# Stores of whole tiles issued by SyncE instead of ScalarE in a decode-attention backward kernel

## The chip, the cores and the metric

The kernel runs on one core of a Trainium2 chip. The metric is the device time of one execution in microseconds (us). Of three runs of the kernel before, the median is 1286.4 us, the lowest 1285.06 and the highest 1288.95.

## The reference

Softmax attention with one query row a head, and its gradients. There are B x H = 2 x 32 = 64 heads, 8192 keys a head, and D = 128; all arrays are bf16.

```
def _fwd_reference(q, k, v):
    scale = q.shape[-1] ** -0.5
    scores = jnp.einsum("bhqd,bhkd->bhqk", q, k) * scale
    p = _softmax(scores, axis=-1)
    return jnp.einsum("bhqk,bhkd->bhqd", p, v)

def reference(q, k, v, grad_out):
    ...
    _out, _vjp = jax.vjp(_f, q, k, v)
    _grads = _vjp(grad_out)
    return (_out, *_grads)
```

So for each head the kernel reads K and V (2 MB each) and writes dK and dV (2 MB each): dV is the outer product of the weights p with grad_out, dK that of the weights' gradient dS with q. The output and dq are one row of 128 values a head.

## The kernel before

A head's K and V lie in SBUF as tiles `kt` and `vt` of 128 partitions x 64 rows x 128 values, 16 KB a partition, 2 MB in all. Each of the two has five buffers (`UNITS = 5`, line 67).

`load(h)` (line 97) issues two DMAs from SyncE (the profile calls it SP), K first, then V; each fills a whole tile. Five heads are loaded ahead of the loop.

The main loop (from line 353) makes 65 rounds. Round h does two things interleaved in eight steps j of two halves: the scores of head h (y in the code) and the gradients of head p = h - 1 (x).

- For head h, TensorE transposes K (steps 0 to 3) and V (steps 4 to 7) in groups of eight 128 x 128 blocks into PSUM (`transposes`, line 113). ScalarE copies each group to SBUF (line 120); in two of the sixteen halves VectorE does (line 118). TensorE then multiplies the copies with q or grad_out (line 136).
- For head p, TensorE sums the weighted rows (line 241) in steps 0 to 3, and VectorE writes the outer products (`outer`, line 271) over the tile that has been read: `outer(p, w, i)` fills the i-th quarter of tile `kv[1 - w]`. With w = 0 this is dV over V (steps 1 to 3), with w = 1 dK over K (steps 3 to 6).

`store(h, w)` (line 328) then writes the whole tile to HBM with one DMA of 2 MB, issued by ScalarE (line 331). In round h the dV store of head p is issued at step 4 and the dK store at step 7, behind what the program has put in ScalarE's queue before: an engine's queue is served in order, and a store that must wait holds the evictions behind it. The last head is stored in halves of 1 MB.

At step 7, behind the dK store, the program writes `load(h + 3)`. That load takes a buffer of an earlier head and so waits until that head's store has landed. As SyncE has only loads to issue, nothing but such waits holds it.

Every 13th head (6, 19, 32, 45, 58) has its dV stored otherwise: `store_by_fifteen` (line 289) issues 24 small stores from GpSimd (POOL in the profile, line 299), mixed with very small copies (`turn`, line 285). Its rows go to fifteen of the sixteen DMA engines.

The order of instructions on each engine is that of the program (`tc.manual_schedule`, line 353); the framework adds the waits, assigns buffers, and gives each DMA a completion counter.

Of the kernel before, what the change touches and what calls it, by code (L numbers as in the profile page):

```python
# [23 lines left out]
def kernel(  # L24
# [11 lines left out]
    nc = tc.nc  # L36
# [40 lines left out]
    dk_v = out_2.rearrange("b h (p n) d -> (b h) p n d", n=NT)  # L77
    dv_v = out_3.rearrange("b h (p n) d -> (b h) p n d", n=NT)
# [16 lines left out]
    heads = [Head() for _ in range(BH)]  # L95
# [193 lines left out]
    def store_by_fifteen(h, w):  # L289

        dst, src = (dv_v, dk_v)[w][h], heads[h].kv[1 - w]

        def rows(lo, n, step=4, size=8192):
            own = slice(lo, lo + step * (n - 1) + 1, step)
            nc.gpsimd.dma_start(out=dst[own], in_=src[own], max_dma_last_dim=size)  # L299

        def fifth(r):
            rows(16 + r, 2, step=32)

        for r in range(4):

            if r == 1:
                fifth(r)
                turn(14)
            rows(52 + r, 11)
            rows(r, 4, size=16384)  # L310
            if r == 0:
                fifth(r)
                turn(3)
            elif r == 3:
                turn(10)
                fifth(r)
                turn(9)
            else:
                turn(5)
            rows(20 + r, 3)  # L320
            if r == 2:
                fifth(r)
                turn(14)
            rows(96 + r, 8)
            rows(32 + r, 4, size=16384)
            turn(5)

    def store(h, w, a=0, b=NT):
        if (2 * h + w) % RARE == RARE // 2 - 1:
            return store_by_fifteen(h, w)  # L330
        nc.scalar.dma_start(out=(dv_v, dk_v)[w][h][:, a:b, :], in_=heads[h].kv[1 - w][:, a:b, :])

    def outer_and_store(h, w, i):

        outer(h, w, i)
        if h == BH - 1 and i % 2:
            store(h, w, (i - 1) * CH, (i + 1) * CH)
# [15 lines left out]
    with tc.manual_schedule():  # L353
        for h in range(min(UNITS, BH)):
            load(h)
        for h in range(BH + 1):
# [4 lines left out]
            for j in range(NS):  # L361
# [24 lines left out]
                if x and p < BH - 1 and j in (4, 7):  # L386
                    store(p, j // 7)
# [49 lines left out]
```

## Time and profile before

| | |
|---|---|
| median of three runs | 1286.4 us |
| span of the profiled execution | 1285.1 us |
| PE, share busy | 83% |
| ACT, share busy | 71% |
| DVE, share busy | 69% |
| HBM read / written | 268.47 / 268.47 MB |
| mean rate of the DMA engines | 420 GB/s |
| DMA issues by ScalarE | 125 of whole or half tiles, 0.34 us each |
| K load, V load: median to landing | 22.9, 31.5 us |
| dK store, dV store by ScalarE: median to landing | 26.9, 21.9 us |

The profile is one execution. Its page cuts the span into 40 slices of 32.1 us; for each it gives the busy share of the DMA engines in tenths and the rate in GB/s. Queue q1 is SyncE's, q10 ScalarE's, and q0 (software_dynamic) GpSimd's. "From issue to landing" runs from the instruction that issues a DMA to its completion. ACTq and SPq are the sequencers of ScalarE and SyncE, which issue DMAs; the engine itself is not busy meanwhile. A wait is put down to whatever came last before the waiting instruction ran; "issue" is time for which the profile shows no such thing.

### The profile page before, as it was taken

How to read it: one execution, taken by the hardware profiler on the slowest of the kernel's cores; microseconds unless marked ns; L12 is line 12 of the kernel's file. 1: busy time of each engine (PE TensorE's matmuls, PEld its weight loads, DVE VectorE, ACT ScalarE, POOL GpSimd, SP SyncE). 2: the span in 40 equal slices, each digit the busy share in tenths (PEclk: the TensorE clock that was granted, in tenths of full speed). 3: DMA queues.
4: the chain of work that ended last, by engine and by line, in shares of the span. 5: the costliest groups of instructions: out<-in, count | busy, mean ns of one | idle time of the engine just before them, and what ended most of it. 6: DMA issues, size and time to landing. Idle time of an engine off the chain costs nothing.

```text
span 1285.1 us, 42433 instructions
## 1 busy us (share of the span) xinstructions
PE 1060.3 (83%) x18948; PEld 877.3 (68%) x18948; DVE 883.8 (69%) x1511; ACT 909.3 (71%) x1043; POOL 105.8 (8%) x193
## 2 busy tenths in 40 slices
PE   5999888848998799499997984999889849899983
PEld 4777777637777677477776774777767737777772
DVE  1887777737787486378875773787767636778775
ACT  5877778737887586488875774877767736788771
POOL 1000111000002110000021200000111000001120
PEclk9999999969999697799996897998979877999996
DMA  9999999999999999999999999999999999999998
GB/s 396 418 426 428 426 426 425 423 431 427 426 426 426 413 424 427 423 427 425 428 426 399 427 426 418 428 427 428 419 403 426 425 419 391 428 429 425 425 424 336
DMA packets 43879, 539.69 MB, mean 420 GB/s; under 512 B 10192, under 2 KB 10192, under 8 KB 10192
## 3 DMA queue, kind: packets, MB, share of 16 engines
q1 hardware_dynamic: 18432, 268.44, 49.5%
q10 hardware_dynamic: 18320, 258.02, 47.4%
q0 software_dynamic: 6944, 10.51, 2.2%
q8 instruction: 148, 2.42, 0.7%
q14 instruction: 35, 0.29, 0.1%
HBM read 268.47 MB, written 268.47 MB: 418 GB/s over the span
## 4 chain that ended last, share of the span: by engine, by line
PE 40%; DMA 26%; ACT 19%; DVE 11%; issue 3%; ACTq 0%; DVEq 0%; SPq 0%
PE tp L113 23%; ACT ev L120 18%; DMA vt<-in_v_dram 9%; DVE ev L118 9%; DMA out_dram<-vt 9%; PE acc L241 9%; DMA kt<-in_k_dram 4%; PE sm L136 4%; DMA out_dram<-kt 3%; PE dp L206 1%; PE dp L136 1%; PE c L259 1%; DMA nat<-in_grad_out_dram 1%; ACT E_f L175 1%; PE sm L170 1%
## 5 line engine op out<-in xcount | busy, mean ns | idle before, releaser
L120 ACT CAST ev<-tp 128x1024 bf16<-128x1024 f32 x896 | 881.2, 1024 | 335.7 <-PE tp L113 232.3
L113 PE MATMUL tp<-ident_bf,vt 128*128 128x128 bf16 x4096 | 327.4, 225 | 134.7 <-ACT ev L120 121.6
L113 PEld LDWEIGHTS <-vt 128*128 128x128 bf16 x4096 | 268.9, 100 | 167.3 <-issue 153.2
L113 PE MATMUL tp<-ident_bf,kt 128*128 128x128 bf16 x4096 | 335.9, 228 | 17.2 <-DMA kt<-in_k_dram 6.5
L113 PEld LDWEIGHTS <-kt 128*128 128x128 bf16 x4096 | 249.4, 101 | 131.5 <-issue 123.2
L136 PEld LDWEIGHTS <-ev 128*128 128x128 bf16 x8192 | 324.4, 98 | 2.2 <-issue 0.2
L271 DVE TENSOR_TENSOR kt<-qd,dS 128x2048 bf16<-128x2048 bf16 x256 | 310.0, 1212 | 0.0
L271 DVE TENSOR_TENSOR vt<-qd,P 128x2048 bf16<-128x2048 bf16 x256 | 295.8, 1216 | 0.0
L118 DVE CAST ev<-tp 128x1024 bf16<-128x1024 f32 x128 | 156.7, 1224 | 186.4 <-PE tp L113 179.4
L136 PE MATMUL dp<-doT_all,ev 128*128 128x1 bf16 x4096 | 178.5, 164 | 0.1
L136 PE MATMUL sm<-qT_all,ev 128*128 128x1 bf16 x4096 | 176.0, 164 | 0.0
L299 POOL DMA_DIRECT2D out_dram<-vt x120 | 67.0, 560 | 1032.7 <-DVE vt L271 832.1
L241 PE MATMUL acc<-vt,wz 128*32 128x512 bf16 x1024 | 109.3, 418 | 17.8 <-DVE wz L186 17.8
L241 PE MATMUL acc<-kt,wz 128*32 128x512 bf16 x1024 | 103.4, 396 | 0.1
L172 DVE TENSOR_SCALAR negm<-sm 128x1 f32<-128x1 f32 x64 | 9.8, 154 | 108.8 <-PE sm L170 108.8
L241 PEld LDWEIGHTS <-wz 128*32 128x32 bf16 x2048 | 52.8, 93 | 32.1 <-DVE wz L186 22.7
L285 POOL DMA_DIRECT2D spare<-in_q_dram x57 | 34.1, 598 | 121.1 <-DMA out_dram<-vt 107.0
L206 PE MATMUL dp<-ld,ones_f 128*128 128x2 f32 x128 | 25.8, 271 | 21.0 <-DVE ld L193 20.9
L206 PEld LDWEIGHTS dp<-ld,ones_f 128*128 128x128 f32 x128 | 20.6, 202 | 31.1 <-DVE ld L193 31.0
L160 DVE TENSOR_REDUCE mp<-sm 128x1 f32<-128x64 f32 x64 | 14.4, 225 | 36.9 <-PE sm L136 36.9
L211 DVE RECIPROCAL rl_all<-dp 128x1 f32<-128x1 f32 x64 | 10.7, 168 | 32.0 <-PE dp L206 32.0
L170 PE MATMUL sm<-gm,ones_f 1*128 1x1 f32 x128 | 25.8, 268 | 0.0
(42 smaller groups left out, 310.5 us busy)
## 6 DMA issues: line engine op xcount, KB each, us to landing
kt<-in_k_dram SPq DMA_DIRECT2D x64, 2048.0 KB, 22.9
vt<-in_v_dram SPq DMA_DIRECT2D x64, 2048.0 KB, 31.5
out_dram<-kt ACTq DMA_DIRECT2D x63, 2048.0 KB, 26.9
out_dram<-vt ACTq DMA_DIRECT2D x58, 2048.0 KB, 21.9
out_dram<-vt POOLq DMA_DIRECT2D x20, 176.0 KB, 23.2
out_dram<-vt POOLq DMA_DIRECT2D x40, 64.0 KB, 23.0
out_dram<-vt POOLq DMA_DIRECT2D x20, 128.0 KB, 22.6
out_dram<-vt ACTq DMA_DIRECT2D x2, 1024.0 KB, 10.9
```

What stands on the lines that cost most here:

```text
L113: nc.tensor.matmul(tp[:, i, :], lhsT=x.kv[w][:, n, :], rhs=ident_bf[:], start=True, stop=True)
L118: nc.vector.tensor_copy(out=ev[:], in_=tp[:])
L120: nc.scalar.copy(out=ev[:], in_=tp[:])
L136: nc.tensor.matmul((x.dp if w else x.sm)[:, n : n + 1], lhsT=ev[:, i, :], rhs=col, start=True, stop=True,)
L160: nc.vector.reduce_max(out=x.mp[:], in_=x.sm[:, 0:NT], axis=AX.X)
L170: nc.tensor.matmul(mb, lhsT=ones_f[0:1, :], rhs=x.gm[:], start=True, stop=True)
L175: nc.scalar.activation(out=x.E[:], in_=x.sm[:, 0:NT], func=ACT.Exp, bias=negm[:], scale=scale, accum_out=x.ld[:, 0:1],)
L206: nc.tensor.matmul(x.lsum, lhsT=ones_f[:], rhs=x.ld[:], start=True, stop=True)
L241: nc.tensor.matmul(acc[32 * g : 32 * g + 32, :], lhsT=wz[w][k][:, n // 4, :], rhs=rows[:, n : n + 4, :].rearrange("p n d -> p (n d)"), sta ...
L271: nc.vector.tensor_tensor(out=x.kv[1 - w][:, n : n + CH, :].rearrange("p n (d t) -> p n d t", t=2), in0=row.unsqueeze(1).to_broadcast([P, ...
L285: nc.gpsimd.dma_start(out=two(spare[0:n, :])[:, :, i : i + 2], in_=two(q_rows[0:n, :])[:, :, 0:2])
L299: nc.gpsimd.dma_start(out=dst[own], in_=src[own], max_dma_last_dim=size)
```

## The change

One line of `store`: the DMA that stores a whole tile (and the halves of the last head) is issued by SyncE, in the place where the program has it. SyncE's queue then holds, for each round, the dV store, the dK store, and the two loads, in this order. The loads of q and grad_out at the start and the stores of the two small outputs at the end stay with ScalarE, and the stores by fifteen engines with GpSimd.

```
     def store(h, w, a=0, b=NT):
         if (2 * h + w) % RARE == RARE // 2 - 1:
             return store_by_fifteen(h, w)
-        nc.scalar.dma_start(out=(dv_v, dk_v)[w][h][:, a:b, :], in_=heads[h].kv[1 - w][:, a:b, :])
+        nc.sync.dma_start(out=(dv_v, dk_v)[w][h][:, a:b, :], in_=heads[h].kv[1 - w][:, a:b, :])
```

More of the change, by code (lines that the diff above doesn't have):

```diff
@@ L330, in store @@
             return store_by_fifteen(h, w)
-        nc.scalar.dma_start(out=(dv_v, dk_v)[w][h][:, a:b, :], in_=heads[h].kv[1 - w][:, a:b, :])
+        nc.sync.dma_start(out=(dv_v, dk_v)[w][h][:, a:b, :], in_=heads[h].kv[1 - w][:, a:b, :])
     def outer_and_store(h, w, i):
```

## The prediction

> **What bounds the kernel now.** First the page's DMA rows by slice, then its DMA queues, then the stages in windows, then who waits on the store and load queues.
>
> ```profile
> DMA  9999999999999999999999999999999999999998
> GB/s 396 418 426 428 426 426 425 423 431 427 426 426 426 413 424 427 423 427 425 428 426 399 427 426 418 428 427 428 419 403 426 425 419 391 428 429 425 425 424 336
> DMA packets 43879, 539.69 MB, mean 420 GB/s; under 512 B 10192, under 2 KB 10192, under 8 KB 10192
> ...
> q1 hardware_dynamic: 18432, 268.44, 49.5%
> q10 hardware_dynamic: 18320, 258.02, 47.4%
> ```
>
> The 16 DMA engines are taken from end to end, and the rate has a ceiling: four long windows (300 to 400, 540 to 640, 800 to 900, 1100 to 1180 us) give 427 GB/s each. 539.69 MB at 427 GB/s are 1263.9 us of a span of 1285.1 us. So transfers bound the kernel, and the 21 us above that floor are all there is to win: the first two slices and the last fall short of 427 by 31 + 9 + 91, or 131 / 427 x 32.1 = 9.9 us, and the slices between by 149 in sum, 11.2 us.
>
> Where the inner part is lost, by windows (length; busy of PE, PEld, DVE, ACT, POOL; PE clock; DMA share; GB/s):
>
> ```profile
> 531.00:539.00 8.00, 4.19 (x54) 3.98 (x54) 1.29 (x2) 4.59 (x7) 0.00 (x0) 0.50 1.02 410
> ...
> 676.00:688.00 12.00, 4.00 (x52) 3.79 (x52) 1.93 (x3) 4.39 (x7) 2.34 (x5) 0.55 0.92 354
> ...
> 938.00:950.00 12.00, 6.41 (x92) 6.00 (x88) 3.49 (x5) 5.75 (x8) 2.57 (x5) 0.58 0.93 368
> ```
>
> The shortfall against 427 times the length: 0.3, 2.0 and 1.7 us. In the same way 418 to 428 (382 GB/s) 1.1, 791 to 801 (393) 0.8, 921 to 929 (395) 0.6, 1051 to 1062 (390) 0.9, 1074 to 1088 (351) 2.5. Together **9.9 us**, nearly all of the 11.2.
>
> What happens there, in ScalarE's timeline (a store is issued, then an eviction runs that had been idle for the time in brackets):
>
> ```profile
> 533.31 0.34 ACTq L331 DMA_DIRECT2D out_dram<-vt  x1
> 533.74 1.93 ACT L120 CAST ev<-tp 128x1024 bf16<-128x1024 f32 x2 [14.96 <-DMA vt<-in_v_dram]
> ...
> 682.50 0.34 ACTq L331 DMA_DIRECT2D out_dram<-vt  x1
> 682.94 1.93 ACT L120 CAST ev<-tp 128x1024 bf16<-128x1024 f32 x2 [7.87 <-issue]
> ```
>
> and in the chain of waits, in order of time:
>
> ```profile
> 502.64 30.59 DMA vt<-in_v_dram
> ...
> 762.78 30.33 DMA vt<-in_v_dram
> ```
>
> The load of V issued at 502.64 lands at 533.23, and the store of another tile is issued at 533.31. Likewise 762.78 + 30.33 = 793.11 and a store at 793.18; 246.85 + 26.57 = 273.42 and 273.49; 1023.33 + 30.29 = 1053.62 and 1053.69. No data joins the two; I infer a completion counter that both use in turn. A store held at the head of ScalarE's queue holds the evictions behind it, so TensorE stops, the next store is late, and then the next load. The waits on ScalarE put down to loads or to "issue" with such a store ahead are 17.3, 15.0, 15.7, 16.0, 7.8, 7.9 and 5.1 us, 85 us. They cost the end only the dips, since one head without waits takes 17.3 us (stores of V at 198.30 and 215.59) and its four transfers 4 x 2.097 MB / 427 GB/s = 19.6 us (4.9 each).
>
> SyncE's waits (total, times, longest) show what paces the loads, buffers becoming free:
>
> ```profile
> SPq L104 <- DMA out_dram<-kt: 888.6, 57, 40.5
> SPq L104 <- DMA out_dram<-vt: 211.6, 21, 11.9
> ```
>
> **The change part by part.**
> *Removed from ScalarE:* 125 issues (63 + 58 + 2 + 2) of 0.34 us are 42 us of its queue, and the held stores 85 us. Both lie beside the transfers, 19.6 against 17.3 us per head; without that cover they would be worth up to 127 us, here 0 by themselves.
> *Added to SyncE:* as many issues. Four per head are 1.4 us of 19.6, and it otherwise only waits: 0.
> *The dips:* a counter's former user is now always an older transfer of the same queue, and a store that waits holds no eviction. Bounds: 0 (the dips return by another road) to -9.9 us. I take **-8**, four fifths, since the last window (1074 to 1088) follows an earlier hold by one round of loads and may have a part that I can't assign.
> *The order of transfers:* SyncE now issues V store, K store, K load, V load for each head. What queues behind a wait there is every later transfer. (a) In most heads a K load waits for the K store of the head before; behind that store stand two loads and two stores, 4 x 4.9 = 19.6 us, so the queue doesn't run dry. The stores wait for their outer products, which come at the pace of the compute; and that waits for no load, since round h issues the loads of round h + 3, two whole rounds (2 x 17.3 = 34.6 us) ahead, and they land in 23 to 32 us. (b) In the five stretches after a store by fifteen engines the V buffer of that head comes back late, and loads come singly (171.40, 181.69, 192.28 us): the V load waits for the V store of its own round. Only the K store and K load, 9.8 us, then stand behind it. The answer takes 1.0 us from issue to the first bytes (issue at 0.74, first traffic at 1.7 us), and the slowest DMA engine lags: the last 1 MB stores took 11.0 us to land, of which data 2.5 and start 1.0, the rest at most 7.5. 9.8 - 1.0 - 7.5 = +1.3 us in hand: I take 0. As the other bound I let the lag grow by a third, to 10 us: 10 + 1.0 - 9.8 = 1.2 us for each of the 21 waits counted above, +25.
> *Loads and stores in one queue:* not in this trace. Loads alone ran at 426 GB/s (38 to 42 us), stores then loads at 421 and 431 (60 to 66, 66 to 72). The first store after loads alone brought 373 GB/s for 4 us (42 to 46), 0.5 us; the store at 273.49 brought none (426, then 434). So a turn costs between 0 and 0.5 us, x 62 heads = 0 to +31. I take 0, by the later row, since both directions were then already running.
> *GpSimd's stores:* unchanged in number. They share the engines with one queue instead of two and should end sooner than now (144 to 252 us for the first); nothing waits for that: 0.
> *The end:* last four half stores 10.9 to 11.0 us to landing as before: 0, within 2 us.
>
> Sum against the profiled execution: 1285.1 - 8 = 1277.1. That execution lies 1.3 us below the median of the three runs, 1286.4; so the median should fall to 1278.4, **say 1279 us**.
>
> **The rivals.**
> *No change (1286).* The dips' cause is the imbalance among DMA engines, not held stores; then the work of the slowest decides and the order of issue nothing. For it: DMA share 1.00 at 393 GB/s in 791 to 801. Against it: shares of 0.92 and 0.93 in the windows shown and 0.90 in 1074 to 1088, where engines stood idle. The Trainium skill's rule in "DMA: Bandwidth & Descriptors" (Rules for kernel authors) says that spreading transfers over SP, ACT and GpSimd gains no bandwidth, as all run on the same 16 engines, and saves only issue time. By it the way back costs none, 1286. The rows of 426 and 427 GB/s agree on the rate; the rule says nothing of held evictions.
> *Slower by turns (1310).* All engines now read together for two transfers and write together for two. Place: each first store after a pair of loads. Price: the 0.5 us of 42 to 46; 62 x 0.5 = 31, 1279 + 31 = 1310. It decides from 0.13 us a turn (8 / 62) on. For it: that window, with ScalarE busy for all of it, so nothing was late. Against it: 273.49. The same page (Two DMAs through the same engine are not ordered) has transfers of one queue start in order but pipelined, reads and writes being separate; by that a turn is free.
> *Slower by a queue run dry (1304).* Place: the V load of case (b). The price is the bound of 25 us, 1279 + 25; it decides from a lag of 8.8 us on. For it: V store and V load are both behind one wait now. Against it: the lag is the sum of two queues' unfairness, of which one goes.
>
> **How the numbers follow.** Forecast 0.50, no change 0.17, turns 0.18, dry 0.15. What a measurement can tell from no change is about 0.3%, 3.9 us (1282.5 to 1290.3). So faster 0.50, same 0.17, slower 0.33. The forecast's own range is 1275 (the 9.9 us and 2 at the end) to 1283; the whole one goes from 1273 to 1312, over the centres of both slower cases.
>
> **What would show it.** Right: no ScalarE wait of over 5 us behind a store, interior slices all at 423 or more, waits on SyncE for stores with DMA share at 1.00. Turns: every slice lowered alike, to some 417, with share at 1.00. Dry: share below 0.97 in the slices after 144, 400, 660, 905 and 1180 us. The forecast falls if GB/s drops in slices that stand at 426 now.

## The result, and the profile after

The changed kernel takes 1295.9 us (median of four runs, 1293.3 to 1297.1), the kernel before, run beside it, 1287.7 us (1285.1 to 1289.5). The ratio is 1.0061, with a 95% interval of 1.0043 to 1.0078: **slower by 0.6%, some 8 us**, where 0.6% less was forecast. The profiled execution has a span of 1293.4 us, against 1285.1 us.

From the page of the changed kernel: the DMA rate by slice (a slice is now 32.3 us) and the DMA queues (packets, MB, share of the 16 engines' span).

```profile
GB/s 396 420 427 429 426 423 426 424 429 426 427 427 425 410 418 410 420 427 427 428 423 408 395 408 421 429 426 428 427 422 387 410 411 428 427 429 427 420 400 320
DMA packets 43878, 539.68 MB, mean 417 GB/s; under 512 B 10192, under 2 KB 10192, under 8 KB 10192
...
q1 hardware_dynamic: 36432, 526.40, 96.8%
q0 software_dynamic: 6944, 10.51, 2.2%
...
q10 hardware_dynamic: 320, 0.07, 0.0%
```

The stores have moved: SyncE's queue holds 526 MB, ScalarE's almost nothing. Between the losses the rate is still 427, so loads and stores in one queue don't lower every slice alike. What is new are three groups of low slices, the 14th to 17th (420 to 550 us), the 22nd to 24th (679 to 776 us) and the 31st to 33rd (970 to 1070 us). They follow the second, third and fourth store by fifteen engines. The single low slices of before (399, 403, 391) are gone or lie in these groups.

ScalarE's largest wait (total, times, longest) and SyncE's first four:

```profile
ACT ev L120 <- PE tp L113: 329.8, 236, 9.4
```

```profile
SPq L104 <- DMA out_dram<-kt: 690.5, 56, 19.3
SPq L104 <- DMA out_dram<-vt: 257.2, 17, 16.4
SPq L331 <- DVE vt L271: 105.5, 18, 20.5
SPq L331 <- DVE kt L271: 89.7, 36, 15.5
```

No eviction waits behind a held store any more: the 85 us of such waits are gone, and nearly all that ScalarE waits for is TensorE. The waits have gone to SyncE. The first two lines are loads waiting for a buffer, as before. The last two are new: a store waits for its outer product, and every load behind it waits too.

The first group of low slices, in windows (length; busy of PE, PEld, DVE, ACT, POOL; PE clock; DMA share; GB/s) and in SyncE's timeline (start, us, instruction):

```profile
417.00:447.00 30.00, 26.66 (x507) 21.83 (x503) 22.81 (x41) 23.22 (x29) 8.05 (x14) 1.00 1.01 424
447.00:460.00 13.00, 8.32 (x161) 7.30 (x160) 7.92 (x11) 8.68 (x11) 0.00 (x0) 0.96 0.94 362
488.00:500.00 12.00, 8.70 (x175) 7.66 (x171) 8.71 (x12) 9.46 (x12) 0.00 (x0) 1.00 1.00 393
```

```profile
449.46 0.34 SPq L104 DMA_DIRECT2D vt<-in_v_dram  x1
449.89 0.73 SPq L331 DMA_DIRECT2D out_dram<-vt  x1
450.67 0.51 SPq L331 DMA_DIRECT2D out_dram<-kt  x1
454.29 0.34 SPq L104 DMA_DIRECT2D kt<-in_k_dram  x1
469.55 0.34 SPq L104 DMA_DIRECT2D vt<-in_v_dram  x1
```

At 449.46 us a V load starts that had waited; the next V store and K store were ready and leave within 1.2 us behind it. What it waited for is seen in the landings. Each DMA of 2 MB is split over the 16 engines, and the trace has one completion event for each. This table is counted from them; the lead is the time from the first engine's landing to the last's.

```
DMA       issued   first lands  last lands   lead
V store   417.69       437.7       449.40    11.7
K store   419.54       442.6       454.24    11.6
K load    433.39       447.9       459.55    11.6
V load    449.46       457.3       464.64     7.3
```

The V load waited for the V store issued at 417.69, which landed at 449.40. Behind that store only a K store and a K load had been issued. The quickest engine had finished both at 447.9, 1.5 us before the V load was even issued. So the quick engines ran dry, DMA share fell to 0.94, and the lead fell from 11.6 to 7.3 us. That is the place of case (b). In the first such stretch (188 to 250 us) the lead was 6 to 8 us, and no slice is low.

The shortfall against 427 GB/s by stages, worked out from the 40 slices as in the prediction (us):

| | slices 1, 2 | 3 to 20 | 21 to 37 | last three |
|---|---|---|---|---|
| before | 3.0 | 2.2 | 8.7 | 7.2 |
| changed | 2.9 | 4.3 | 11.6 | 10.7 |

The 8.3 us by which the two spans differ are 5.0 in the interior and 3.5 at the end.

### The profile page after: what moved, and what is told of

It is laid out like the page before. It is cut to its first block, busy times and chain, and to the rows that moved or that the text cites. A ratio compares the mean times of both kernels' runs of the same rounds, so it can differ in the third digit from the quotient of the medians.

```text
span 1293.4 us, 42287 instructions
## 1 busy us (share of the span) xinstructions
PE 1098.9 (85%) x18948; PEld 902.5 (70%) x18948; DVE 883.8 (68%) x1511; ACT 906.4 (70%) x1043; POOL 106.0 (8%) x193
## 4 chain that ended last, share of the span: by engine, by line
DMA 41%; PE 14%; ACT 3%; DVE 3%; issue 1%; SPq 0%; ACTq 0%; DVEq 0%
DMA kt<-in_k_dram 26%; DMA out_dram<-kt 15%; PE tp L113 8%; PE acc L241 3%; ACT ev L120 3%; PE sm L136 1%; DVE kt L271 1%; DVE ev L118 1%; DVE vt L271 1%; PE dp L136 0%; PE dp L206 0%; DVE accsb L252 0%; PE c L259 0%; PE sm L164 0%; SPq L104 0%
## 5 line engine op out<-in xcount | busy, mean ns | idle before, releaser
L113 PE MATMUL tp<-ident_bf,kt 128*128 128x128 bf16 x4096 | 373.1, 244 | 88.5 <-DMA kt<-in_k_dram 82.5
L113 PEld LDWEIGHTS <-kt 128*128 128x128 bf16 x4096 | 276.1, 109 | 220.9 <-issue 133.1
L113 PE MATMUL tp<-ident_bf,vt 128*128 128x128 bf16 x4096 | 313.5, 219 | 48.3 <-ACT ev L120 38.1
L136 PEld LDWEIGHTS <-ev 128*128 128x128 bf16 x8192 | 331.0, 99 | 2.1 <-issue 0.2
L113 PEld LDWEIGHTS <-vt 128*128 128x128 bf16 x4096 | 259.2, 98 | 81.7 <-issue 73.5
L241 PE MATMUL acc<-vt,wz 128*32 128x512 bf16 x1024 | 123.3, 472 | 7.0 <-DVE wz L186 6.7
L241 PE MATMUL acc<-kt,wz 128*32 128x512 bf16 x1024 | 106.3, 408 | 0.4 <-DVE wz L186 0.4
L160 DVE TENSOR_REDUCE mp<-sm 128x1 f32<-128x64 f32 x64 | 14.4, 225 | 57.8 <-PE sm L136 57.8
L211 DVE RECIPROCAL rl_all<-dp 128x1 f32<-128x1 f32 x64 | 10.7, 168 | 34.5 <-PE dp L206 34.5
L154 ACT CAST qd<-pb 128x1024 bf16<-128x1024 f32 x16 | 16.2, 1012 | 12.3 <-PE pb L146 12.3
## 6 DMA issues: line engine op xcount, KB each, us to landing
out_dram<-vt POOLq DMA_DIRECT2D x20, 176.0 KB, 12.1
out_dram<-vt POOLq DMA_DIRECT2D x20, 128.0 KB, 12.2
out_dram<-vt SPq DMA_DIRECT2D x2, 1024.0 KB, 13.5
```

The lines of the kernel that those rows point to most:

```text
L113: nc.tensor.matmul(tp[:, i, :], lhsT=x.kv[w][:, n, :], rhs=ident_bf[:], start=True, stop=True)
L136: nc.tensor.matmul((x.dp if w else x.sm)[:, n : n + 1], lhsT=ev[:, i, :], rhs=col, start=True, stop=True,)
L154: nc.scalar.copy(out=qd[:], in_=pb[:])
L160: nc.vector.reduce_max(out=x.mp[:], in_=x.sm[:, 0:NT], axis=AX.X)
L241: nc.tensor.matmul(acc[32 * g : 32 * g + 32, :], lhsT=wz[w][k][:, n // 4, :], rhs=rows[:, n : n + 4, :].rearrange("p n d -> p (n d)"), sta ...
```

## The experiments

Two theories stood at first. A: the dry queue at the V load, as above. B: loads and stores in one queue cost by themselves. C, that engines drift apart whoever waits for what, was stated with them. The first four runs led to D, which the later ones test: one of the 16 engines is slower, and **the quick ones can lead it by no more than the transfers issued behind the store for which the next load waits**. Each run was timed beside the kernel before, and its ratio is to that. The lead is meant as in the table above.

**1. The V load written a round later**

`load` issues K and, for the first five heads alone, V; `load_v` issues V.

```
     def load(h):
...
+        load_one(h, 0)
+        if h < UNITS:
+            load_v(h)
...
                 if x and p < BH - 1 and j in (4, 7):
                     store(p, j // 7)
+                if j == 4 and UNITS <= h + 2 < BH:
+                    load_v(h + 2)
```

> Stores by SyncE as in the changed kernel, but the V load of a head is written one round later, behind the next round's V store, so that SyncE no longer stops at a V load that waits for the V store issued just before it. Theory A (the queue runs dry where the V load waits for its own round's V store, in the stretches after a store by fifteen): the slices at 395 to 411 GB/s between 400 and 1220 us go back to 420 or more, and the time falls from 1296 to 1279 to 1284 us. Theory B (loads and stores in one queue cost by themselves, wherever the waits lie): 1293 to 1298 us, with the same low slices. Theory C (the stretches after a store by fifteen lose time because the 16 DMA engines have drifted apart, whoever waits for what): 1287 to 1296 us, low slices there at the level of the kernel before.

1289.5 us; ratio 1.0008 (0.9995 to 1.0021). Its rate by slice:

```profile
GB/s 396 418 424 428 426 423 426 426 428 427 429 428 424 424 428 428 428 427 429 427 419 411 425 428 426 427 416 422 427 393 427 428 425 416 414 425 413 397 425 298
```

The first group of low slices is gone (424 to 428), the second has shrunk to 419 and 411, the third to a single slice of 393. That is 6.4 us of the loss, so A names the place rightly. But it ends level with the kernel before, not at 1279 to 1284. The time lies in C's range, but C had the low slices stay: neither A nor C alone. From 840 us on other slices are low (416, 422, 414, 413), and the end is worse (397, 425, 298).

**2. Six buffers for V**

```
-            kvp.tile([P, NT, D], BF16, name="vt", tag="vt"),
+            kvp.tile([P, NT, D], BF16, name="vt", tag="vt", bufs=UNITS + 1),
...
-    spare = const.tile([16, 1024], BF16)
+    spare = const.tile([16, 512], BF16)
```

> Stores by SyncE as in the changed kernel, with six buffers for V instead of five (the small target tile of the very small copies is halved to make room), so that a V load finds a buffer that came free a round earlier. Theory A (dry queue at the V load): no V load waits for the V store of its own round, also after a store by fifteen; 1278 to 1284 us. Theory B (one queue costs by itself): 1293 to 1298 us. Theory C (drifted engines): 1287 to 1296 us.

1292.8 us; 1.0037 (1.0024 to 1.0049). SyncE's first wait is now `DMA out_dram<-kt`, 910.4 us in 56 times; no wait for a V store is left among the large ones. The same 427 or so up to the 19th slice, then low slices and an end of 276. So taking the V wait away gives 3 to 6 us, by whichever way, and something else holds the rest. The 3.3 us between this run and the first I can't explain.

**3 and 4. No store by fifteen engines, stores on SyncE and on ScalarE**

```
-        if (2 * h + w) % RARE == RARE // 2 - 1:
+        if False:
```

> Stores by SyncE, all of them whole tiles: no store by fifteen engines and none of the very small copies. Read against the same kernel with the stores on ScalarE (next run). Theory A: the V loads never meet the V store of their own round, so SyncE minus ScalarE lies between -8 and +2 us. Theory B (one queue costs by itself): SyncE minus ScalarE is +6 to +10 us as with the stores by fifteen. Both may be slower than the kernel before, as the one DMA engine that the stores by fifteen leave out is not relieved: 63.5 KB... no row gives the size; an estimate of 0 to +25 us.

> Stores by ScalarE as in the kernel before, all of them whole tiles: no store by fifteen engines. The partner of the run before. Theory A: its time is that of the run before within -2 to +8 us, its own held stores included. Theory B: it is 6 to 10 us faster than the run before.

SyncE 1325.5 us, ScalarE 1304.4 us: B's sign, at twice its size, and A fails. Windows of the two, SyncE first:

```profile
100.00:400.00 300.00, 264.65 (x4616) 216.67 (x4616) 215.01 (x368) 219.61 (x252) 0.00 (x0) 0.91 1.01 427
700.00:1200.00 500.00, 429.34 (x7170) 351.54 (x7169) 333.48 (x567) 342.59 (x393) 0.00 (x0) 0.86 1.00 406
```

```profile
100.00:400.00 300.00, 262.95 (x4696) 216.32 (x4696) 219.02 (x373) 223.85 (x259) 0.00 (x0) 0.94 1.01 427
700.00:1200.00 500.00, 430.77 (x7312) 353.37 (x7309) 339.74 (x583) 348.14 (x402) 0.00 (x0) 0.88 1.00 417
```

For 300 us one queue costs nothing: 427 both. It is later that they part, so B is wrong as stated. The landings show when. Median lead of the dK stores (us) in stretches of 100 us from the time given, later runs among them:

```
                        300   400   500   600   700   800   900  1000
before                 13.0   4.2  11.1  16.4   4.8  15.1   4.4   5.0
changed                11.9   8.0  10.7  15.1   8.4  11.9  12.2   9.7
1 late V, SyncE        11.0  11.3  14.3  18.0  15.3  17.9  14.7  17.6
3 no fifteen, SyncE    16.6  18.4  18.3  18.8  18.5  18.7  18.8  19.3
4 no fifteen, ScalarE  24.2  28.2  28.1  28.7  28.1  28.4  27.7  28.7
5 four V, SyncE         8.3   2.9   5.6   7.8   2.9   7.5   6.3   4.7
6 four V, ScalarE       6.3   8.7   2.4   6.7   7.0   6.8  12.7  12.7
9 K on SyncE, V ScalarE 15.5 17.8  16.3  17.3  18.4  17.9  19.2  17.2
```

In run 3 the lead grows by about 1 us a head and then stands at 18 to 19 us. SyncE's queue has four transfers behind the store that the K load waits for: 4 x 4.9 = 19.6 us, less the 1.0 us of a restart, 18.6. In run 4 the lead of the stores goes on to 28. A waiting load there holds no store: with the next round's two stores issued as well it would be six transfers, 28.4, which fits. In the changed kernel's dry stretches (400, 700, 1000) it is cut to 8 to 10, by the same count of two transfers 8.8. Once the lead stands still, the rate falls.

Two things in the landings limit this reading. First, with the stores on ScalarE there are two busy queues, each with a lead of its own, and the table has the stores' alone. Around the dip at 676 to 688 us of the kernel before, the lead of the K stores falls from 15.4 to 3.3 us while that of the K loads stays (14.1, then 13.8); in run 4 the lead of the K loads is 7 and that of the V loads 9 to 10. An estimate from the landings of both queues is 4.9 us times the mean number of 2 MB transfers that the first engine has landed and the last has not. From 420 us on it is 18 us in run 4 and 17 in run 3: the engines drift no further apart on two queues. Why run 3 then falls to 406 GB/s and run 4 only to 417 stays open.

Second, D's one slow engine is not what most runs show. Of run 3's K store issued at 1000.5 us, fifteen engines land within 2.7 us of the first, and one at 18.2. Of the changed kernel's K store issued at 419.54, seven land within 3.8 us, and nine between 7.9 and 11.6. One engine stands alone without the stores by fifteen; with them, nine are late together.

**5 and 6. Four buffers for V, on SyncE and on ScalarE**

`load` issues K and, for the first four heads alone, V.

```
+        if h < UNITS - 1:
+            load_v(h)
...
+        heads[h].kv[1] = kvp.tile([P, NT, D], BF16, name="vt", tag="vt", bufs=UNITS - 1)
...
                     if x and UNITS <= h + 3 < BH:
                         load(h + 3)
+                    if x and UNITS <= h + 4 < BH + 1:
+                        load_v(h + 3)
```

> The suspected wait in every round: stores by SyncE, and only four buffers for V, so that every V load waits for the V store of its own round, with one K store and one K load issued behind that store (two transfers, 9.8 us). Theory D, formed on the first four runs: one DMA engine is slower than the others, and the quick ones can run ahead of it by no more than the transfers issued behind the store that the next load waits for, less about 1 us; at that cap the rate falls. Two transfers cap the lead at 8 to 9 us, four (the run without stores by fifteen) at 18 to 19. The 21 such waits of the changed kernel cost 6.4 us (1295.9 against 1289.5 with the late V load), 0.3 each; some 55 rounds lie behind the point where the lead first reaches 8 us. D: 1289.5 + 55 x 0.3 = 1306, between 1300 and 1315, and the lead never over 9 us. Rival (the loss belongs to the stretches after a store by fifteen engines alone, and not to the wait): 1293 to 1298 us, like the changed kernel.

> The same four V buffers with the stores on ScalarE, where a waiting load holds no store. Theory D: the K store and the next round's stores are still issued behind the V store that the load waits for, so that the lead may grow past 9 us; 1286 to 1294 us, at least 8 us faster than the run before. Rival (what counts is the number of buffers, not whose queue the stores stand in): within 3 us of the run before.

SyncE 1326.0 us, 1.0309 (1.0291 to 1.0327); ScalarE 1286.3 us, 0.9997 (0.9984 to 1.0009). The two kernels differ in the queue of the stores alone. Rates by slice, and what the loads wait for most, SyncE first (line 109 there is line 104 here):

```profile
GB/s 397 400 427 427 426 267 426 428 426 428 421 402 418 332 428 427 428 428 424 406 408 335 425 428 427 428 428 404 411 338 426 427 426 428 417 406 411 337 409 380
```

```profile
SPq L109 <- DMA out_dram<-vt: 889.4, 66, 25.3
```

```profile
GB/s 396 416 427 427 424 421 421 424 427 430 425 427 426 413 425 415 428 429 427 427 426 409 425 405 427 430 427 426 427 422 413 424 418 429 427 427 426 411 416 336
```

```profile
SPq L109 <- DMA out_dram<-vt: 787.3, 56, 35.3
```

The loads wait as long on ScalarE's stores (787 us, up to 35 us) as on SyncE's (889, up to 25). Only on SyncE does it cost, 40 us. So it isn't the wait of a load that is dear, but the stores that stand behind it. The lead on SyncE is never over 10.1 us, about as D has it. The size was wrong, though: 1326 lies outside the 1300 to 1315 expected. The five deepest slices (267, 332, 335, 338, 337) lose 41 us together: there the V load waits for the small stores by fifteen of its own round, which I had not counted. What the other inner slices lose, 13 us, is only 4 more than in the first run, not 16.

**7 and 8. Seven stores by fifteen instead of five**

```
-RARE = 26
+RARE = 18
```

Run 7 is run 1 with this edit, run 8 the kernel before with it.

> Stores by SyncE with the late V load (1289.5 us), and the dV store of every 9th head by fifteen engines instead of every 13th: seven such stores instead of five, so that the slowest engine moves 2 x 131 KB less (2 x 4.9 us). Theory D: the lead of the quick engines stays below 18 us, the low slices from 830 us on go back to 424 or more, and the time falls by 5 to 10 us, to 1280 to 1284. Rival (what is left is the price of loads and stores in one queue, or the small stores cost as much as they relieve): 1287 to 1293 us.

> The kernel before with seven stores by fifteen engines instead of five. If the dips of the kernel before are the quick engines waiting for the slowest one (theory D), there are fewer of them and the time falls a little: 1281 to 1286 us. If the dips are made by stores held on ScalarE by themselves, as the prediction had it, they stay: 1285 to 1290 us.

1289.5 us, 1.0024 (1.0016 to 1.0033), and 1288.3 us, 1.0011 (0.9997 to 1.0024). Both miss what D expected, and lie in the ranges of the other reading. In the first the interior improves (7.3 us short, against 9.3 in run 1), but the lead still reaches 15 to 20 us, and the last three slices lose 13.2. Taking work off one engine is no gain, so "the slowest engine decides" is too simple. It would fit the nine late engines above, since this edit takes work off one.

**9. Half of the change: dK stores on SyncE, dV stores on ScalarE**

```
-        nc.sync.dma_start(out=(dv_v, dk_v)[w][h][:, a:b, :], ...
+        (nc.scalar, nc.sync)[w].dma_start(out=(dv_v, dk_v)[w][h][:, a:b, :], ...
```

> Half of the change: the dK stores by SyncE, the dV stores by ScalarE as before. In the stretches after a store by fifteen engines the V load still waits for the V store of its own round, but the next V store no longer stands behind that load: three transfers (K store, K load, next V store) instead of two, so the lead of the quick engines may reach 3 x 4.9 - 1 = 13.7 us there. Theory D (the lead is capped by what is issued behind the awaited store): the slices of the changed kernel at 387 to 411 GB/s after 400 us rise to 415 or more; 1286 to 1291 us. Rival (it is the store in the loads' queue as such): half of the loss of the changed kernel stays or more, 1291 to 1296 us.

1290.4 us, 1.002 (1.0002 to 1.0038): within D's range, with the slices from 420 to 550 us at 421 to 425. But the lead is 15 to 19 us, not at most 13.7, so my count of transfers is wrong for this kernel, and the slices from 190 to 390 us stand at 412 to 421. It shows that half the stores in the loads' queue cost about half (3.9 us of 8.2), and not why.

**10. The control of the first run: late V load, stores on ScalarE** (the diff of run 1, with line 331 as before)

> The control of the first run: the late V load with the stores on ScalarE. Theory D: a waiting V load holds only loads there, so writing it later changes nothing; 1284 to 1290 us. Rival (the late V load is a gain of its own, which the first run showed together with the loss of the change): 1278 to 1283 us.

1286.3 us, 0.9988 (0.997 to 1.0005). The late V load is no gain of its own. On SyncE the same edit takes 6.4 us off.

**11 and 12. One more store by fifteen near the end**

```
-        if (2 * h + w) % RARE == RARE // 2 - 1:
+        if (2 * h + w) % RARE == RARE // 2 - 1 or (h, w) == (61, 0):
```

Run 11 is run 7 with this edit, run 12 the kernel before with it.

> The run with the late V load and seven stores by fifteen engines (1289.5 us; its last three slices lose 13.2 us against 427 GB/s, the kernel before 7.2), with one more such store near the end, that of dV of head 61. If what it loses at the end is the slowest engine finishing after the others (8.0 us behind the median engine at the last store), 4.9 us of its work go to the others: 1284 to 1286 us, faster than the kernel before by up to 0.2%. Rival (the small stores cost at the end what they relieve): 1288 to 1293 us.

> The kernel before with the same extra store by fifteen engines at head 61. Its slowest engine ends 4.3 us behind the median one, so at most 4 us are to be had: 1283 to 1286 us. Rival: no change or slower, 1286 to 1290 us.

1290.5 us, 1.0022 (1.0006 to 1.0038), and 1299.6 us, 1.0095 (1.0065 to 1.0124). The first is what the rival expected; the second lies beyond even the rival's 1290. On ScalarE the small stores are simply late; the program's end waits for them:

```profile
SPq L432 <- DMA out_dram<-vt: 67.5, 1, 67.5
```

No version is faster than the kernel before by more than its interval.

## Why the prediction was wrong, step by step

**Right.** ScalarE's issues and held stores lay beside the transfers: 85 us of waits vanished and no time with them. Loads and stores in one queue are free by themselves: 427 GB/s between the losses, and for 300 us of run 3. So the rival of turns falls. Step (a) holds in its count: with 19.6 us of queue behind a store the engines run dry only when the lead comes to 18.6, which run 3 reaches and stays at. One clause of it fails, that the compute "waits for no load": TensorE waits 82.5 us for K loads, against 6.5 before (the last column is its idle time and what ended most of it). What that costs no run separates. GpSimd's stores end sooner, the first group at 203 us instead of 249.

```profile
L113 PE MATMUL tp<-ident_bf,kt 128*128 128x128 bf16 x4096 | 373.1, 244 | 88.5 <-DMA kt<-in_k_dram 82.5
```

**First failed step: "I take 0" for the V load of case (b).** The place, the waits and the two transfers behind them were as written there, and the test with a late V load prices them at 1295.9 - 1289.5 = 6.4 us (six V buffers, run 2, at 3.1). The size that failed is the lag, "at most 7.5", read from the end of the run. It isn't one number. It grows by some 1 us a head and is 6 to 8 us in the first stretch after a store by fifteen, but 11.7 in the second. The +1.3 us in hand were then 9.8 - 1.0 - 11.7 = -2.9. The rival of the dry queue was this mechanism, priced four times too high (25), since the first wait of a stretch cuts the lead and the next ones pay less (2.0 us lost in 447 to 460, 1.0 in 488 to 500).

**Second failed step: "I take -8" for the dips.** Without case (b), run 1 has the held stores gone and nothing gained: +2.1 us by the medians, +1.0 by the ratio (-0.6 to +2.7). By stages against the kernel before: slices 3 to 20 win 1.7 us (2.2 to 0.5), slices 21 to 37 nothing (8.7 to 8.8), and the last three lose 4.9 (7.2 to 12.1). The step booked the dips as the price of the held stores, and the runs show such holds without a dip. The longest in the kernel before, 17.3 us up to 273.9 us, has none. In run 6 ScalarE idles four times behind a held store, for 11.3 to 13.0 us, and the rate stays at 426 to 431. First a window of the kernel before, then run 6's waits on ScalarE (three lines, four times) and the windows of the four:

```profile
256.00:272.00 16.00, 1.49 (x33) 1.35 (x31) 2.20 (x3) 0.68 (x1) 0.00 (x0) 0.65 1.00 429
```

```profile
ACT ev L125 <- DMA vt<-in_v_dram: 23.9, 2, 12.1
ACT ev L125 <- issue: 13.0, 1, 13.0
ACT qd L159 <- DMA vt<-in_v_dram: 11.3, 1, 11.3
```

```profile
287.00:307.00 20.00, 9.30 (x110) 7.08 (x111) 7.00 (x16) 4.05 (x4) 0.00 (x0) 0.58 1.00 428
546.00:566.00 20.00, 9.27 (x123) 7.20 (x122) 7.91 (x16) 4.30 (x6) 0.00 (x0) 0.59 1.00 426
807.00:827.00 20.00, 9.71 (x114) 7.15 (x111) 6.71 (x15) 5.05 (x6) 0.00 (x0) 0.55 1.01 431
1066.00:1086.00 20.00, 10.29 (x130) 7.96 (x131) 8.24 (x17) 4.93 (x5) 0.00 (x0) 0.57 1.01 430
```

And of the 9.9 us booked, 3.1 lay in windows without a hold (921 to 929 and 1074 to 1088 us). So a hold by itself costs no rate.

What the holds with a dip have in common is engines that have drifted apart. By the estimate over both queues, in the 20 us before each hold ends, the drift is 10.3 to 14.4 us at the six holds with a dip in the kernel before, 8.5 at the one without, and 6.9 to 9.0 at the four of run 6. Run 8's six holds fall in line: 6.4 and 9.0 us at the two without a dip (430 and 427 GB/s), 10.8 to 12.2 at the other four (405 to 421). That is near the rival "no change", whose share of 0.92 I had read against it. No run varied the drift alone, so that it makes the dips is argued, not shown. So is what run 1 pays instead: its lead stays at 11 to 18 us from 300 us on, with a little lost in many slices and more at the end.

**Third: the end, "0, within 2 us".** It is +3.5 us: the last half stores take 13.5 us to land instead of 10.9 (last line here; from the DMA issues: count, KB each, median us to landing).

```profile
out_dram<-vt POOLq DMA_DIRECT2D x20, 176.0 KB, 12.1
...
out_dram<-vt SPq DMA_DIRECT2D x2, 1024.0 KB, 13.5
```

Together: -8 forecast, +2.1 found without case (b), which has the end in it; 0 forecast, +6.4 found for case (b); the sum +8.5 against the +8.2 measured. The sum has to agree, since both terms are differences to run 1; what the runs add is how it divides. By the marks set beforehand, "dry" was right in three of its five places: low slices after 400, 660 and 905 us, each with a window at a share of 0.94 (447 to 460, 700 to 712, 972 to 985 us). After 144 us the share stays at 1.01 (425 GB/s to 252 us), and after 1180 us it is 0.98 at 401 GB/s (1220 to 1240 us).

The Trainium skill, "DMA: Bandwidth & Descriptors" (Issuing engines are not separate DMA queues), says that issuing from several engines at once saves only the issue time. The trace agrees for the first 400 us of runs 3 and 4 (427 and 427 GB/s) and disagrees where the stores stand behind loads that wait for long: 1326.0 against 1286.3 us in runs 5 and 6.

## What to carry to other kernels

A queue that issues both loads and stores stops both at the first wait. Before moving stores into it, count for each waiting load what is issued behind the store that it waits for, and compare that with the lead of the quickest DMA engine over the slowest, taken from the landings in the stretch in question and not from the end of the run. If the stores must stand there, write the load behind the next store: here that gave back 6.4 of 8 us. Before booking a dip in the rate as the price of a wait that stands beside it, look for the same wait without a dip: here the profile before had one, the longest of all.

## What the runs showed of the hardware

- The 16 engines don't keep step under equal work: in run 3 the quickest gains about 1 us a head on the slowest, and one engine lands the last store 9.2 us after all the other fifteen. The Trainium skill, "DMA: Bandwidth & Descriptors" (Latency and other measured facts), calls two engines usually slower in traces and, as a best guess, links it to GpSimd's DMAs. The records here carry no engine numbers, and run 3 has only two very small GpSimd DMAs, so this doesn't settle which it is or why.
- At a standing lead the lost rate isn't idleness but longer packets: share 1.00 at 406 GB/s. In run 3 a packet of 16 KB took 617 ns on average from 300 to 400 us and 656 ns from 1100 to 1200 us, with a median of 611 ns in both: a few packets take much longer. Why stays open.
- GpSimd's small stores landed in 12 us instead of 22 to 23, with one busy queue beside them instead of two. The Trainium skill, "DMA: Bandwidth & Descriptors" (Queues, rings and completion order), has each engine take turns among the queues that have work. The trace agrees.
